# Sums of PV kept feature-major through DRAM for seven of eight branch segments of a gated mix of two infini-attentions

## The chip, the cores and the metric

The kernel runs on one core of a Trainium2 chip. The metric is the device time of one execution in microseconds (us); the median of several executions is compared. TensorE (PE in the profile, PEld for its weight loads) multiplies matrices into eight PSUM banks of 128 partitions by 512 floats. VectorE (DVE), ScalarE (ACT) and GpSimd (POOL) work element by element. SyncE (SP) issues every transfer between DRAM and on-chip memory (SBUF); sixteen DMA engines carry them out. Each engine works through its own queue in the written order and waits on semaphores.

## The reference, cut to what matters

Two branches, A and B, do the same with their own weights on the same x (2048 tokens, 640 features, 32 heads of 20). The tokens are cut into four segments of 512. In a segment every head has causal attention; from the second segment on a memory part is mixed in, built from the keys and values of the segments before.

```python
for s in range(N):                       # N = 4 segments, L = 512
    qs, ks, vs = q[:, :, s], k[:, :, s], v[:, :, s]
    logits = einsum("bhqd,bhkd->bhqk", qs, ks) * scale + mask
    p = softmax(logits)
    a_dot = einsum("bhqk,bhkd->bhqd", p, vs)
    pq = phi(qs)
    num = einsum("bhld,bhde->bhle", pq, M)
    den = einsum("bhld,bhd->bhl", pq, z)[..., None] + 1e-6
    o = g * (num / den) + (1.0 - g) * a_dot          # g = sigmoid(beta), per head
    pk = phi(ks)
    M = M + einsum("bhld,bhle->bhde", pk, vs)
    z = z + einsum("bhld->bhd", pk)
out_branch = concat(o) @ wo
...
g = sigmoid((x * gate_w).sum(-1))        # per token
return g * out_A + (1 - g) * out_B
```

## The kernel before

A **branch segment** t = 0 to 7 is one segment of one branch: t // 2 is the segment s, t % 2 the branch. Its work on TensorE is 10 projections for q and k (one per 128 features, `job_qk`), the projection of v in two halves (`job_v`), the attention of eight units of four heads each (unit i = 8t + u), and five output projections (`job_o`). q, k, v and o weights and their inputs are split in a high and a low part, and three products (high by high, low by high, high by low) stand for one in full precision.

TensorE's array is used as two halves of 64 rows. A planner in the Python code keeps a clock of its own for both halves and for the other engines, and writes the instructions in the order in which it starts them. Projections are the filling (`fill_gen` walks through the list `jobs`); the scores of a unit are strewn in by `RULES`, a table with a row of numbers for each of 66 steps: the order of score pieces (S: queries by keys, for the maxima; T: keys by queries, for the exponentials), how far they spread over the step, how loaded VectorE may be before late work is put off, and waits. The list of late units (`late`) holds turns and the memory's products.

For one unit the chain is: maxima of S in VectorE (line 1109), turned and sent into the query tile; T with the maxima in two more rows; exponential in ScalarE (line 1204); causal cut in GpSimd (1205); then `pv_unit` (line 1232), which multiplies v with the exponentials. Its bank holds, for each of four heads, 20 rows of sums and one row with the denominator, by 512 tokens: features stand in partitions, so it is **feature-major**. The bank is copied to a row tile (line 1259). A row tile is one of 28 places of 128 by 512 floats, shared by all.

Then `fin_unit` turns that tile to tokens: eight transposes on TensorE (line 838, four per half, against an identity), after which tokens stand in partitions. There the denominator of a head is one column, so VectorE multiplies it by the gates (`gq`, 128 by 4 by 32 for a branch segment, line 1298), inverts it (1299) and multiplies the sums (1300). In segment 0 this goes straight into the tile `O` of finished tokens; later the memory part already stands in `O` (`mem_unit`, 800 to 817), and GpSimd adds (1310). When the units that a group of 128 features needs are done, `o_transpose` turns them back to feature-major with eight more transposes (line 838 again, input `O`), and the high and low parts for the output projection are made from the bank (1328). The output of branch A goes to DRAM as `part`, and branch B's is added to it.

The order of jobs in the window of t is: the rest of q, k and v of t, the five output projections of t − 1, then the first five projections of t + 1.

Of the kernel before, what the change touches and what calls it, by code (L numbers as in the profile page):

```python
# [12 lines left out]
F32 = mybir.dt.float32  # L13
# [5 lines left out]
P = 128  # L19
# [23 lines left out]
def tile_gated_mix_infini_attn(  # L43
# [376 lines left out]
    def window_jobs(t):  # L420
        got = [(t, kind, m) for kind, m in (TAIL if t else [("q", 1), ("k", 1), ("v", 0), ("q", 2), ("k", 2)] + TAIL[2:])]
        if t > 0:
            got += [(t - 1, "o", m) for m in range(KT)]
        if t < 7:
            got += [(t + 1, kind, m) for kind, m in HEAD]
# [1185 lines left out]
```

## Time and profile before

| what | us |
|---|---|
| median of three runs | 1027.75 |
| lowest and highest | 1026.51, 1028.1 |
| the profiled execution's own time | 1026.22 |
| span of its profile | 1024.5 |
| TensorE busy | 1015.8 |
| VectorE, ScalarE, GpSimd busy | 760.0, 659.3, 581.5 |

The span is the time from the first to the last instruction of the profiled execution. Busy times of the engines overlap. In a group's row, the number before the bar counts instructions; behind it stand the busy time in us and the mean of one in ns, and then the idle time of that engine just before them with what ended it. In rows of waits stand the waiting engine and line, what it waited for, the total, the times and the longest. In the rows of stretches, the share of the DMA engines and GB/s come last, after the granted clock. In the timeline the start and the length come first; a name such as `bank<-ident,O` is written tile and read tiles.

### The profile page before, as it was taken

What the parts mean: (1) busy time and instruction counts of PE and PEld (TensorE: products, weight loads), DVE (VectorE), ACT (ScalarE), POOL (GpSimd) and SP (SyncE); (2) the same over time, 40 slices, a digit from 0 to 9 for tenths busy, and PEclk for the clock granted to TensorE, in tenths of its full rate; (3) what the DMA queues carried; (4) which work ended last, traced back from release to release, by engine and by line L of the source; (5) the groups of instructions that cost most, each with busy time, mean ns of one, the idle gap of its engine ahead of it and who ended that gap; (6) DMA issues with size and microseconds to landing.
All of it is one profiled execution on the core that took longest, in us unless ns stands there. A gap on an engine that the chain in (4) does not pass through costs nothing.

```text
span 1024.5 us, 31917 instructions
## 1 busy us (share of the span) xinstructions
PE 1015.8 (99%) x11780; PEld 873.7 (85%) x11780; DVE 760.0 (74%) x2725; ACT 659.3 (64%) x1337; POOL 581.5 (57%) x1043
## 2 busy tenths in 40 slices
PE   9999999999999999999999999999999999999998
PEld 7988888988988889889898988989889888888876
DVE  4777787678768788676887668967687867778764
ACT  6375777677655675675756458566675656666672
POOL 4364655665444765566646456565774646645561
PEclk9999999999999999999999999999999999999999
DMA  8996866666675676764766468684775865957431
GB/s 274 305 281 186 280 191 211 194 187 219 181 225 163 196 247 197 232 177 145 264 175 221 132 189 276 196 249 140 205 245 157 263 187 164 286 160 225 134 109 53
DMA packets 110028, 207.97 MB, mean 203 GB/s; under 512 B 12464, under 2 KB 16560, under 8 KB 109872
## 3 DMA queue, kind: packets, MB, share of 16 engines
q1 hardware_dynamic: 109872, 205.93, 66.4%
q8 instruction: 93, 1.52, 0.6%
q14 instruction: 63, 0.52, 0.2%
HBM read 131.43 MB, written 73.40 MB: 200 GB/s over the span
## 4 chain that ended last, share of the span: by engine, by line
PE 95%; DMA 2%; DVE 1%; ACT 1%; POOL 0%; issue 0%; SPq 0%; ACTq 0%; DVEq 0%
PE bank L690 54%; PE bank L1232 13%; PE bank L1122 7%; PE bank L1212 7%; PE bank L838 4%; PE bank L800 3%; PE bank L878 3%; DMA qd<-row 2%; PE bank L1147 1%; PE bank L736 1%; PE bank L328 1%; DMA wst<-in_a_wo_dram 1%; PE bank L1051 0%; DVE bank L1109 0%; DVE row L1036 0%
## 5 line engine op out<-in xcount | busy, mean ns | idle before, releaser
L1109 DVE CUSTOM_DVE_ANT_0 bank<-bank,tri 128x256 f32<-128x256 f32 (+3 forms) x1024 | 475.2, 519 | 135.3 <-PE bank L1122 107.6
L690 PE MATMUL bank<-row,wh 64*128 64x512 f32 x2308 | 528.3, 404 | 0.0
L1204 ACT ACTIVATE p<-bank 128x512 f32<-128x512 f32 x596 | 328.7, 601 | 142.0 <-PE bank L1212 110.1
L1205 POOL TENSOR_SCALAR_AFFINE_SELECT p<-p 128x256 f32<-128x256 f32 (+1 forms) x596 | 215.5, 371 | 228.3 <-ACT p L1204 214.7
L690 PEld LDWEIGHTS bank<-row,wh 64*128 64x128 f32 x2308 | 330.0, 186 | 8.9 <-issue 0.6
L690 PE MATMUL bank<-row,wl 64*128 64x512 f32 x1154 | 308.7, 399 | 0.0
L517 POOL TENSOR_TENSOR wl<-wst,wh 128x640 fp32r<-128x640 f32 x115 | 179.8, 1566 | 81.8 <-ACT wh L515 81.0
L690 PE MATMUL bank<-wvh,row 64*128 64x320 f32 x1280 | 198.4, 316 | 0.1
L690 PEld LDWEIGHTS bank<-row,wl 64*128 64x128 f32 x1154 | 180.3, 186 | 4.4
L1122 PE MATMUL bank<-kst,qst 60*128 60x384 f32 (+3 forms) x1024 | 176.8, 318 | 1.3 <-ACT row L1259 0.6
L1212 PE MATMUL bank<-qst,kst 62*128 62x384 f32 (+3 forms) x1024 | 173.1, 318 | 0.2 <-ACT row L854 0.2
L690 PEld LDWEIGHTS bank<-wvh,row 64*128 64x128 f32 x1280 | 161.3, 185 | 3.1 <-issue 1.0
L1232 PE MATMUL bank<-p,vst 128*32 128x512 f32 (+3 forms) x1952 | 148.3, 429 | 0.0
L1109 DVE DVE_READ_ACCUMULATOR2_ANT mx<- 128x1 f32 x1024 | 144.2, 141 | 0.0
L1122 PEld LDWEIGHTS bank<-kst,qst 60*128 60x128 f32 x1024 | 131.1, 185 | 8.6 <-DVE mx L1109 1.3
L1212 PEld LDWEIGHTS bank<-qst,kst 62*128 62x128 f32 x1024 | 128.9, 186 | 6.8 <-DVE mx L1109 1.0
L1232 PEld LDWEIGHTS bank<-p,vst 128*32 128x32 f32 x1952 | 59.3, 109 | 85.1 <-issue 65.3
L515 ACT CAST wh<-wst 128x640 fp32r<-128x640 f32 x119 | 86.4, 743 | 37.6 <-PE bank L690 26.2
L690 PE MATMUL bank<-wvl,row 64*128 64x320 f32 x640 | 109.9, 311 | 0.0
L690 PEld LDWEIGHTS bank<-wvl,row 64*128 64x128 f32 x640 | 87.7, 185 | 0.3
L492 POOL TENSOR_TENSOR wvl<-wst,wvh 128x640 fp32r<-128x640 f32 (+1 forms) x48 | 64.1, 1341 | 17.1 <-ACT wvh L489 16.5
L838 PE MATMUL bank<-ident,row 64*128 64x64 f32 x752 | 72.7, 225 | 0.8 <-ACT row L1204 0.8
(100 smaller groups left out, 1224.5 us busy)
## 6 DMA issues: line engine op xcount, KB each, us to landing
qd<-row SPq DMA_DIRECT2D x120, 256.0 KB
kd<-row SPq DMA_DIRECT2D x120, 256.0 KB
qst<-qd SPq DMA_DIRECT2D x128, 240.0 KB
kst<-kd SPq DMA_DIRECT2D x128, 240.0 KB
wst<-in_a_wq_dram SPq DMA_DIRECT2D x20, 320.0 KB
wst<-in_a_wk_dram SPq DMA_DIRECT2D x20, 320.0 KB
wst<-in_b_wq_dram SPq DMA_DIRECT2D x20, 320.0 KB
wst<-in_b_wk_dram SPq DMA_DIRECT2D x20, 320.0 KB
```

Of the source, the lines that this page charges most:

```text
L492: put("G", 0.77 * n, lambda: nc.gpsimd.tensor_tensor(out=wl[:, a:b, :], in0=w3, in1=r32(wh[:, a:b, :]), op=ALU.subtract), end, prio=4)
L515: put("A", 0.625, lambda: nc.scalar.copy(wh, w3), lambda: put(lo_eng, lo_cost, lambda: lo.tensor_tensor(out=wl, in0=w3, in1=r32(wh), op=AL ...
L517: lambda: lo.tensor_tensor(out=wl, in0=w3, in1=r32(wh), op=ALU.subtract), end, prio=3), prio=6)
L690: return nc.tensor.matmul(bank_of, lhsT=w[ROWS[half]], rhs=x_[ROWS[half]], start=start, stop=stop)
L800: return nc.tensor.matmul(pm[:, a - h0:c - h0, :].rearrange("p h e -> p (h e)"), lhsT=r32(pqTs[t, m][ROWS[half], P * n:P * (n + 1)]), rhs= ...
L838: return nc.tensor.transpose(px[:, n, r], block(n)[r], ident[r, r])
L1109: put("D", w / 960.0 + 0.105, lambda: nc.vector.tensor_tensor_reduce(out=sc[:, off:off + w], in0=sc[:, off:off + w], in1=tri[:, L - w:], s ...
L1122: lane_ops[half].append((mm(w), lambda pair=pair, qb=qb, off=off, w=w, r=r, sc=sc: nc.tensor.matmul(sc[:, off:off + w], lhsT=q[r, pair, P ...
L1204: put("A", 0.483, lambda: nc.scalar.activation(pt, sc, AF.Exp, scale=SCALE), lambda: (bank.give(sc), put("G", 0.15 + 0.105 * len(todo), la ...
L1205: "G", 0.15 + 0.105 * len(todo), lambda: nc.gpsimd.affine_select(out=blocks, in_=blocks, pattern=[[0, len(todo)], [1, P]], base=0, channel ...
L1212: lane_ops[half].append((mm(w), lambda pair=pair, kb=kb, off=off, w=w, r=r, sc=sc: nc.tensor.matmul(sc[:, off:off + w], lhsT=k[r, pair, P ...
L1232: nc.tensor.matmul(po[32 * j:32 * j + 32, P * kb:], lhsT=vst[t % 2][:, kb, h * E1:h * E1 + 32], rhs=pts[i, n, f][0][:, off:off + w], start ...
```

## The change

For t = 0 to 6 the sums are not turned to tokens. `send_dot` sends the tile of a unit to DRAM while it is feature-major: four transfers of 20 rows to `dots` and one of the four denominator rows to `dens`. When four units (16 heads) are there, `reciprocals` loads their denominators as 128 partitions by 64, multiplies by the head's factor (`gcol`, one number per partition) and the token gate (`row_gate`, laid out in the same way by three small transfers for each branch segment), inverts, and sends them back to `recs`. One transfer from DRAM to DRAM (`wide`) repeats every head's row 20 times, so that it lies as the features do. `mix` loads a tile of 128 features from `dots` and from `wide` and multiplies them, on VectorE or GpSimd. In segment 0 the high and low parts are made of the product at once. In later segments the memory part, which is still made by tokens, is turned by `o_transpose`, and VectorE adds it to the product. The last branch segment (t = 7) works as before.

Beside that, the gates by tokens for the sums (`gqd`) are made for t = 7 only; the first two projections of t + 1 stand ahead of the output projections of t − 1; a second wait (`wait2`) is in the table of rules for the second half of a turn; and the table has new rows.

```diff
@@ RULES (most rows of the table differ; one of them)
-        0: "TSTSTSTSTS 0.969 2.38 0.27 8 0.0 1.6",
+        0: "STTSTSSTST 0.902 2.38 0.24 8 0.0 0.78 1",
...
+    dots = [dram.tile([D, L], F32, name=f"dots{i}") for i in range(7)]
+    dens = [dram.tile([H, L], F32, name=f"dens{i}") for i in range(7)]
+    recs = [dram.tile([H, L], F32, name=f"recs{i}") for i in range(7)]
+    wide = [dram.tile([D, L], F32, name=f"wide{i}") for i in range(7)]
...
     def window_jobs(t):
+        ahead = [(t + 1, kind, m) for kind, m in HEAD] if t < 7 else []
+        got += ahead[:2]
         if t > 0:
             got += [(t - 1, "o", m) for m in range(KT)]
-        if t < 7:
-            got += [(t + 1, kind, m) for kind, m in HEAD]
+        got += ahead[2:]
...
+    def row_gates(s):
+        for b in range(2):
+            t = 2 * s + b
+            if t < 7:
+                row_store.want(1, lambda r, t=t, b=b, s=s: dma(0.3, lambda: nc.sync.dma_start(
+                    out=rowg[t].rearrange("n p -> p n")[:, :, None], in_=gate[b][:, NB * s:NB * (s + 1), None]),
+                    lambda: spread(r, t), prio=8 if s == 0 else marks[16 * s] - 10, some=True), prio=t)
...
             def end():
                 bank.give(po)
+                if t < 7:
+                    send_dot(i, oT)
+                    return
                 oTs[i] = oT
                 later(1, 0.44, lambda: fin_ok(i), lambda: fin_unit(i))
...
+        one = then_all(5, sent)
+        dma(0.1, lambda: nc.sync.dma_start(out=dens[t][4 * u:4 * u + 4, :], in_=oT[DH::32, :]), one, prio=-1)
+        for j in range(4):
+            dma(0.12, lambda j=j: nc.sync.dma_start(
+                out=dots[t][80 * u + DH * j:80 * u + DH * (j + 1), :], in_=oT[32 * j:32 * j + DH, :]), one, prio=-1)
...
+    def reciprocals(t, g, d):
+        rows = slice(16 * g, 16 * g + 16)
...
+        def work():
+            nc.vector.scalar_tensor_tensor(
+                out=d, in0=d, scalar=gcol[t % 2][:, g:g + 1], in1=row_gate[t], op0=ALU.mult, op1=ALU.mult)
+            nc.vector.reciprocal(d, d)
+
+        def written():
+            dma(0.1, lambda: nc.sync.dma_start(
+                out=recs[t][rows, :].rearrange("h (a n) -> (h a) n", n=SPAN), in_=d), widen, prio=-1)
+
+        def widen():
+            dn_store.give(d)
+            dma(1.8, lambda: nc.sync.dma_start(
+                out=wide[t][DH * 16 * g:DH * 16 * (g + 1), :].rearrange("(h e) n -> h e n", e=DH),
+                in_=recs[t][rows, None, :].to_broadcast([16, DH, L])), over, prio=-1)
...
+    def mix(t, k, y, r):
+        def weighed():
+            big.give(r)
+            if t < 2:
+                parts()
+            else:
+                mixed[t, k] = y
+                later(1, 0.44, lambda: all(
+                    (t, n, h) in mem_done for n in range(NB) for h in range(2) if k in mem_tiles(h)), lambda: o_transpose(t, k, parts))
...
+        landed = then_all(2, lambda: anyof(
+            2, weighed,
+            D=(0.605, lambda: nc.vector.tensor_tensor(out=r32(y), in0=r32(y), in1=r32(r), op=ALU.mult)),
+            G=(1.25, lambda: nc.gpsimd.tensor_tensor(out=r32(y), in0=r32(y), in1=r32(r), op=ALU.mult))))
+        dma(0.7, lambda: nc.sync.dma_start(out=r32(y), in_=dots[t][P * k:P * k + P, :]), landed, prio=0)
+        dma(0.7, lambda: nc.sync.dma_start(out=r32(r), in_=wide[t][P * k:P * k + P, :]), landed, prio=0)
```

How it moves instructions is seen best at three places of the built programs. The first is TensorE behind the last PV unit of t = 1. Before, its sums, `row_5270_4569`, are turned into `bank_119` among score pieces (L1122, L1212) and products (L690):

```order
L1122 MATMUL bank_124<-kst_85,qst_81 128x128
L838 MATMUL bank_119<-ident,row_5270_4569 128x64 x2
L690 MATMUL bank_122<-row_3093_2719,wh_132 128x512
L838 MATMUL bank_119<-ident,row_5270_4569 128x64 x2
L690 MATMUL bank_118<-row_3043_2668,wh_128 128x512
L690 MATMUL bank_122<-row_3465_3070,wh_132 128x512
L690 MATMUL bank_118<-row_3093_2719,wh_128 128x512
L1212 MATMUL bank_121<-qst_83,kst_87 128x384
L1212 MATMUL bank_117<-qst_83,kst_87 128x384
L1212 MATMUL bank_121<-qst_83,kst_87 128x128
L838 MATMUL bank_119<-ident,row_5270_4569 128x64 x2
L1212 MATMUL bank_117<-qst_83,kst_87 128x128
```

In the change, the last two rows of that PV unit (now L1261, bank_169) are followed by the memory's update (L907), products (L717) and score pieces (L1241), and no turn reads that unit's sums anywhere:

```order
L1261 MATMUL bank_169<-p_5796_4593,vst_89 32x128
L1261 MATMUL bank_169<-p_5797_4594,vst_89 32x128
L907 MATMUL bank_166<-vst_88,row_5409_4236 128x147
L717 MATMUL bank_168<-row_3412_2767,wh_180 128x512
L907 MATMUL bank_166<-vst_88,row_5409_4236 128x147
L1241 MATMUL bank_163<-qst_80,kst_84 128x512
L1241 MATMUL bank_167<-qst_80,kst_84 128x512
L717 MATMUL bank_168<-row_3444_2785,wh_180 128x512
L907 MATMUL bank_166<-vst_88,row_5409_4236 128x147
```

Eight turns of that unit are gone from the queue, and the bank that they wrote is not taken. The second place is VectorE near the end of t = 1. Before, it weighs a unit's turned sums into the tokens `O_144` between two pairs of maxima (L1109, each with the read of its result):

```order
L1109 ISA bank_122,mx_4888<-bank_122,tri 128x512
L1109 ISA mx_4888 128x1
L901 COPY mt_146<-bank_121 128x147
L1298 TENSOR_TENSOR fw_4937<-bank_124,gqd_141 128x16
L1299 RECIPROCAL fw_4937<-fw_4937 128x16
L1300 TENSOR_TENSOR O_144<-bank_124,fw_4937 128x4x80
L1109 ISA bank_118,mx_4888<-bank_118,tri 128x384
```

In the change, at the end of t = 0, the products of `mix` (L1375) and a low part (L1370) stand there, ahead of the maxima (now L1138):

```order
L1138 ISA mx_3046 128x1
L1375 TENSOR_TENSOR row_3913_3163<-row_3913_3163,row_3914_3164 128x512
L922 COPY mbd_3_78<-bank_164 128x147
L1375 TENSOR_TENSOR row_3918_3165<-row_3918_3165,row_3919_3166 128x512
L1370 TENSOR_TENSOR row_4028_3234<-row_3913_3163,row_4027_3233 128x512
L1138 ISA bank_164,mx_3252<-bank_164,tri 128x512
```

What VectorE waited for there came from TensorE's turn; what it waits for now comes from two transfers. The third place is SP at the same end of t = 0, in the change alone (before, no transfer belongs to this step):

```order
L1306 DMA dens_125<-row_3710_3017 4x512
L1308 DMA dots_118<-row_3710_3017 20x512 x4
L1341 DMA wide_138<-recs_131 320x1x512
L532 DMA wst_173<-in_a_wo_dram 128x640
L554 DMA row_3845_3124<-in_xT_dram 128x512
L554 DMA row_3876_3142<-in_xT_dram 128x512
L611 DMA rowg_148<-gate_91 128x4x1
L1377 DMA row_3913_3163<-dots_117 128x512
L1378 DMA row_3914_3164<-wide_138 128x512
L1377 DMA row_3918_3165<-dots_117 128x512
L1378 DMA row_3919_3166<-wide_138 128x512
```

The loads of sums and widened factors stand behind the widening, and weights, inputs of the next segment and the first sums of t = 1 share the queue with them.

More of the change, by code (lines that the diff above doesn't have):

```diff
@@ L824, in end @@
             mem_done.add((t, n, h))
+            if t < 7 and all((t, nn, hh) in mem_done for nn in range(NB) for hh in range(2)):
+                gq_store.give(gq.pop(t))
         def read():
@@ new lines, in reciprocals, with landed, over @@
+    def reciprocals(t, g, d):
+        rows = slice(16 * g, 16 * g + 16)
+        def landed():
+            put("D", 0.75, work, written, prio=2)
+        def work():
[10 more added lines that the diff above has]
+                in_=recs[t][rows, None, :].to_broadcast([16, DH, L])), over, prio=-1)
+        def over():
+            rec_there.add((t, g))
+            if (t, 1 - g) in rec_there:
+                row_store.give(row_gate.pop(t))
+            dots_ready(t)
+        dma(0.1, lambda: nc.sync.dma_start(
+            out=d, in_=dens[t][rows, :].rearrange("h (a n) -> (h a) n", n=SPAN)), landed, prio=-1)
@@ L1287, in end @@
             fin_done.add(i)
-            if all(8 * t + j in fin_done for j in range(8)):
-                gq_store.give(gq.pop(t))
             for k in range(KT):
@@ L1317, in tile_gated_mix_infini_attn, with o_transpose, add @@
     ot_count = {}
-    def o_transpose(t, k):
+    def o_transpose(t, k, parts=None):
         b = bank.free.pop(0)
         px = b.rearrange("p (n c) -> p n c", c=P)
+        def add():
+            y = mixed.pop((t, k))
+            put("D", 0.605, lambda: nc.vector.tensor_tensor(
+                out=r32(y), in0=b, in1=r32(y), op=ALU.add), lambda: (bank.give(b), parts()), prio=2)
         def got(hi, lo):
@@ L1444, in lane_step @@
         u = seconds[half][0] if seconds[half] else None
[L1445 removed]
+        if u and next_start(half, u["ops"][half][0][0][1])[1] >= u["at"] + (rule["wait2"] if u["turn"] else 0.0):
             return run_second(half, u)
@@ L1512, in rules @@
         if i in RULES:
-            order, rule["span"], rule["calm"], rule["lag"], rule["room"], rule["hold"], rule["wait"] = RULES[i].split()
+            order, rule["span"], rule["calm"], rule["lag"], rule["room"], rule["hold"], rule["wait"], rule["wait2"] = RULES[i].split()
             rule.update({x: float(rule[x]) for x in rule if x != "order"}, order=order)
```

76 lines of the change are left out of this document (59 added, 17 removed), and 111 rows, old and new, of the table RULES.

## The prediction

> **What bounds the kernel now.** I read the page's first part, then the chain that ended last, then the stretches, then who waited for whom.
>
> ```profile
> PE 1015.8 (99%) x11780; PEld 873.7 (85%) x11780; DVE 760.0 (74%) x2725; ACT 659.3 (64%) x1337; POOL 581.5 (57%) x1043
> PE 95%; DMA 2%; DVE 1%; ACT 1%; POOL 0%; issue 0%; SPq 0%; ACTq 0%; DVEq 0%
> by line: PE bank L690 54.1%; PE bank L1232 13.5%; PE bank L1122 7.1%; PE bank L1212 6.9%; PE bank L838 4.4%; PE bank L800 3.1%; PE bank L878 3.0%; DMA qd<-row 1.6%; PE bank L1147 0.8%; PE bank L736 0.7%; PE bank L328 0.6%; DMA wst<-in_a_wo_
> ```
>
> TensorE is busy 99% of the span and its own work makes 95% of the chain. A matmul's record overlaps its neighbours', so 99% alone proves little; the list of TensorE's waits says more.
>
> ```profile
> PE bank L328 <- DVE qst L332: 1.5, 1, 1.5
> PE bank L838 <- ACT row L1204: 0.8, 1, 0.8
> PE bank L1122 <- ACT row L1259: 0.6, 1, 0.6
> PE bank L1122 <- DVE row L854: 0.5, 1, 0.5
> PE bank L1212 <- ACT row L854: 0.2, 1, 0.2
> PE bank L1122 <- ACT p L1204: 0.2, 1, 0.2
> ```
>
> That is the whole list: under 4 us in six waits, and no transfer is in it. The stretches show the same from beginning to end, at full clock.
>
> ```profile
> 0.00:100.00 100.00, 97.67 (x1002) 84.56 (x1004) 67.97 (x233) 57.37 (x116) 50.08 (x84) 1.00 0.86 265
> 100.00:200.00 100.00, 100.00 (x1222) 87.10 (x1222) 74.42 (x273) 71.67 (x148) 60.58 (x116) 1.00 0.73 222
> 200.00:1024.50 824.50, 818.11 (x9563) 702.05 (x9559) 617.58 (x2224) 530.22 (x1074) 470.88 (x845) 1.00 0.64 193
> ```
>
> So the number and price of TensorE's instructions set the time. What leaves its queue shortens the span, as long as what replaces it doesn't make it wait.
>
> **What is removed from TensorE.** A unit of turns is eight transposes, four per row half. Gone are the 56 units that turned PV's sums to tokens (seven of eight branch segments, eight groups of heads each) and ten that turned the finished tokens back in branch segments 0 and 1. Branch segments 2 to 6 still turn their memory part. That is 66 × 8 = 528 of these 1072 rows:
>
> ```profile
> L838 PE MATMUL bank<-ident,row 64*128 64x64 f32 x752 | 72.7, 225 | 0.8 <-ACT row L1204 0.8
> L838 PEld LDWEIGHTS bank<-ident,row 64*128 64x128 f32 x752 | 60.7, 138 | 3.7 <-ACT row L1204 1.1 <-issue 0.8 <-PE bank L838 0.3
> L838 PE MATMUL bank<-ident,O 64*128 64x64 f32 x320 | 34.4, 226 | 0.1
> L838 PEld LDWEIGHTS bank<-ident,O 64*128 64x128 f32 x320 | 27.9, 139 | 3.8 <-issue 2.3 <-PE bank L838 0.5 <-DVE row L657 0.2
> L690 PEld LDWEIGHTS bank<-row,wh 64*128 64x128 f32 x2308 | 330.0, 186 | 8.9 <-issue 0.6 <-ACT row L674 0.4 <-PE bank L690 0.3
> 170.19 0.41 PE L838 MATMUL bank<-ident,O 64*128 64x64 f32 x4
> 170.41 0.39 PE L690 MATMUL bank<-wvh,row 64*128 64x320 f32 x1
> 170.43 0.39 PE L690 MATMUL bank<-row,wh 64*128 64x512 f32 x1
> ```
>
> Three prices. The lowest is the bare slot: in the timeline four turns of one half start at 170.19 and the next products at 170.41 and 170.43, so four take 0.24 us of their half at most, and both halves lose that once: 66 × 0.24 = 15.8 us. The middle is what the chain charges: 4.4% of 1024.5 us is 45.1 us for 1072 turns, 0.042 us each, and 528 × 0.042 = 22.2 us. It holds the time that a turn costs its neighbours as well. The highest counts weight loads: (60.7 + 27.9) × 528 / 1072 = 43.6 us of PEld's 873.7. I take the chain's 22.2, because it alone is measured along what sets the end, and keep 15.8 and 43.6 for the range.
>
> **What the other engines gain and lose.**
>
> ```profile
> L1298 DVE TENSOR_TENSOR fw<-bank,gqd 128x16 f32<-128x16 f32 x64 | 10.9, 171 | 19.7 <-PE bank L838 12.5 <-ACT row L1204 2.9 <-PE bank L1122 1.4
> L1299 DVE RECIPROCAL fw<-fw 128x16 f32<-128x16 f32 x64 | 16.2, 253 | 2.5 <-DVE fw L1298 0.4
> L1300 DVE TENSOR_TENSOR ft<-bank,fw 128x320 f32<-128x320 f32 x48 | 23.6, 492 | 4.8 <-DVE fw L1299 0.5
> L1328 DVE TENSOR_TENSOR row<-bank,row 128x512 fp32r<-128x512 f32 x40 | 27.5, 688 | 15.1 <-ACT row L1328 12.4 <-POOL mt L1134 2.6
> L539 DVE TENSOR_TENSOR row<-row,row 128x512 fp32r<-128x512 f32 x5 | 3.4, 692 | 0.9 <-ACT row L535 0.9
> L539 POOL TENSOR_TENSOR row<-row,row 128x512 fp32r<-128x512 f32 x15 | 19.3, 1298 | 2.3 <-ACT row L535 2.1
> L1310 POOL TENSOR_TENSOR O<-O,ft 128x320 f32<-128x320 f32 x46 | 40.9, 890 | 30.9 <-DVE ft L1300 26.7 <-DVE mw L814 4.1
> ```
>
> VectorE loses 56 × (171 + 253 + 492) ns = 51.3 us of weighing and 35 × 0.688 = 24.1 us of low parts read from a bank. It gets 54 of the 70 new whole-row operations (35 products, 35 low parts) at 0.692 us, 37.4 us; 25 additions of the memory part, 17.2 us; and 14 inversions of 128x64, about 0.17 us for the product and some 0.54 us for the reciprocal (an estimate: 253 ns for 16 columns against 241 for 13 in the same view gives near 5 ns a column), 10 us. The net is some 10 us less. GpSimd loses 40 additions, 35.6 us, and gets 16 whole-row operations at 1.298 us, 20.8 us. ScalarE casts the same 35 tiles from another place. None of them is near TensorE's share, so I cost this at nothing; if it were all on the path it would be a gain, not a loss.
>
> **What is added in transfers.** 417 more (893 become 1310), all issued by SP. In bytes, from the shapes: 9.2 MB of sums written, 9.2 read back, 9.2 of widened factors written and 9.2 read, 1.6 of small ones: 38.4 MB.
>
> ```profile
> q1 hardware_dynamic: 109872, 205.93, 66.4%
> L1038 SPq DMA_DIRECT2D out_dram<-row x5: 332/333/338, 1018.0 to 1020.7; - x5
> L979 SPq DMA_DIRECT2D out_dram<-row x15: 337/349/413, 324.2 to 854.5; - x15
> 281.84 2.29 PE bank L1232 x32
> 14.73 3.66 PE bank L690 x30
> ```
>
> At the same price per byte the queue's share goes from 66.4% to 66.4 × 244.3 / 205.9 = 79%; in the stretch 100 to 200, some 5 MB more takes 0.73 to near 0.88, close to the 0.86 that the first stretch bore. Issuing adds 417 × 0.35 = 146 us to SP, which waits for much of the span. So bandwidth should hold; the length of the path is the question. After a segment's last PV come five transfers in a row: sums and denominators out, denominators in as 128x64, the inverse out, widened in memory, both back in. One transfer of 256 KB takes at most 3.8 us to land (the last is issued at 1020.7, the span ends at 1024.5). Five make 19 us; four more issues, the wider third and the six tiles that hang on the second group of heads add some 8, VectorE's and ScalarE's steps 3: about 30 us. The room for it: branch segment 1's last PV ends at 284.1 (281.84 + 2.29) and its first finished output leaves at 324.2, 40 us later; of that the job's own 30 products take at least 3.7 us. The change puts two jobs of 30 products ahead, 7.3 us more at the price of 3.66 us for 30; their two weight tiles go ahead of the output weights on SP too, in the order in which TensorE needs them. So some 43 us of room at most against 30.
>
> The Trainium skill's page "DMA: Bandwidth & Descriptors", section "Anatomy of one DMA — SWDGE (gpsimd) path", puts a transfer's fixed cost at about 2.0 us, most of it the receipt of the write, plus bytes over 436 GB/s. By it (an estimate) 256 KB take 2.6 us and the five steps 13 us instead of 19, and the chance that the path is late would be smaller than I put it; the section fits another issuing path, and no row of before shows one small transfer alone.
>
> Waiting is what can go wrong. The inversion and the product sit in in-order queues ahead of the maxima (L1109) that free the score banks. Before, these groups waited for transfers:
>
> ```profile
> L515 ACT CAST wh<-wst 128x640 fp32r<-128x640 f32 x119 | 86.4, 743 | 37.6 <-PE bank L690 26.2 <-DMA wst<-in_b_wo_dram 3.0 <-DMA wst<-in_a_wq_dram 2.3
> L489 ACT CAST wvh<-wst 128x640 fp32r<-128x640 f32 (+1 forms) x48 | 31.0, 651 | 5.3 <-DMA wst<-in_b_wv_dram 3.7 <-DMA wst<-in_a_wv_dram 1.5
> L1259 ACT COPY row<-bank 128x512 f32<-128x512 f32 x59 | 34.8, 590 | 55.9 <-PE bank L1232 47.6 <-PE bank L878 3.2 <-DMA qd<-row 2.5
> L854 DVE COPY row<-bank 128x512 f32<-128x512 f32 x8 | 5.5, 691 | 10.0 <-DMA qd<-row 4.4 <-PE bank L1147 2.2 <-PE bank L838 1.6
> ```
>
> They add up to 17.4 us, or 0.0195 us for each of 893 transfers; 417 more make 8 us of engine time, of which VectorE's idle quarter and the banks in reserve hide most. I take 3 us on the path. The bounds are 0 and, at 28 places (14 inversions, 14 groups of products) with 1 us each uncovered, 28 us.
>
> **The table of rules** is new in most rows and moves the order of everything; no row of before prices that. I give it nothing and 5 us either way.
>
> **The sum.** The profiled execution took 1026.22 us (span 1024.5). 1026.22 − 22.2 + 3 = 1007.0. The median of the three runs is 1.5 us above the profiled one, so 1008.5.
>
> **The rivals.**
> - *A larger gain.* Turns cost the products around them more than the chain shows, by holding up their weight loads. For it: the 43.6 us of loads that go. Against it: a product's load is 186 ns beside a slot of 0.122 us, a turn's 138 ns beside 0.06 us in its half, so loads overlap. Between 22.2 and 43.6 I put this case at 33 us saved: 1026.2 − 33 + 3 + 1.5 = 998.
> - *Weight loads are the bound.* Then all 43.6 us come off: 1026.2 − 43.6 + 1.5 = 984. PEld's 85% beside a TensorE that waits for nobody speaks against it. The Trainium skill's page "Trainium Kernel Development and Optimization", section "Best Practices", says that distance to the limit is judged by the busy share of LDWEIGHTS and not by that of matmuls; by that rule this would be the case.
> - *Part is given back.* The path of five transfers is later than its room in each of seven branch segments, by 1.5 us: 10.5 us, about 1019. For it: nothing before is that long. Against it: 43 us against 30; it begins to cost at 1.4 times my path.
> - *Slower.* VectorE stands at the inversion or the product until a transfer lands, the maxima queue behind it, score banks stay taken, TensorE stops. At 28 places it breaks even from 22.2 / 28 = 0.8 us each; at 1.1 us uncovered it costs 31 us: 1026.2 − 22.2 + 31 + 1.5 = 1036. For it: the queue's share near 0.88 early, SP in order with 417 more entries, each able to hold those behind. Against it: 17.4 us of such waits before, none that reached TensorE.
> - *It changes nothing*: the turns' slots were filled anyway by waiting. Against it: six waits on TensorE in all. 1027.
>
> **Chances.** Forecast 0.60 (1000 to 1015), larger gain 0.09, weight loads 0.02, part given back 0.13, no change 0.03, slower 0.13. A measurement of this kernel tells 0.2%, some 2 us, from no change. Faster 0.84, same 0.03, slower 0.13. The range of eight in ten goes from 997 (just under the larger gain) to 1022 (past the partial one): about 0.06 is left out below and 0.14 above.
>
> **What would show it.** Right: TensorE's list still names no transfer, L838's successor has 544 rows and about 23 us of chain, the share of PE in the chain stays above 93%, the queue's share is near 79%. Wrong: TensorE waiting for L1138 (the maxima's new line) or for rows that come from transfers, VectorE's idle time ahead of the inversions and products in tens of us, or stretches in which TensorE's count of instructions falls just where the output projections begin.

## The result, and the profile after

The changed kernel takes 1106.09 us (median of four, 1103.16 to 1109.64) where the kernel before took 1027.92 beside it (1026.51 to 1028.59). The ratio is 1.0764, 95% interval 1.073 to 1.0798: slower, by 78 us, and 98 us above the forecast.

First the page of the changed kernel: span, busy times, packets, the transfer queue (packets, MB, share) and the chain that ended last.

```profile
span 1104.7 us, 31255 instructions
PE 1035.1 (94%) x11252; PEld 877.9 (79%) x11252; DVE 770.5 (70%) x2636; ACT 657.6 (60%) x1334; POOL 574.0 (52%) x1010
DMA packets 142027, 246.50 MB, mean 223 GB/s; under 512 B 26208, under 2 KB 30304, under 8 KB 141872
q1 hardware_dynamic: 141872, 244.50, 75.3%
PE 30%; DMA 6%; DVE 2%; ACT 1%; POOL 1%; issue 1%; SPq 0%; DVEq 0%; ACTq 0%; POOLq 0%
```

TensorE has the 528 instructions fewer that were promised (11,252 for 11,780), but it made 95% of the chain and now makes 30%. Its list of waits, six entries and 3.8 us before, has 28 entries and 64.4 us; its first rows (what waited, for what, total us, times, longest):

```profile
PE bank L1241 <- ACT p L1233: 9.3, 2, 6.3
PE bank L867 <- DVE row L668: 8.3, 1, 8.3
PE bank L1151 <- DVE mx L1138: 5.4, 4, 3.3
PE bank L827 <- ACT vst L957: 4.6, 1, 4.6
```

These are few and long, and entries further down name GpSimd and a transfer too: no one engine is late, several are, for some us at a time. The stretches show when. Two us each: length, TensorE's busy time with its instructions, its granted clock, the DMA engines' share and their GB/s.

```profile
480.00:482.00 2.00, 2.00 (x29) 1.00 1.06 402
482.00:484.00 2.00, 2.00 (x29) 1.00 0.40 148
484.00:486.00 2.00, 2.00 (x36) 1.00 0.31 47
486.00:488.00 2.00, 2.00 (x32) 1.00 0.37 39
488.00:490.00 2.00, 1.48 (x24) 1.00 0.46 8
490.00:492.00 2.00, 0.00 (x0) 0.98 0.47 32
492.00:494.00 2.00, 0.00 (x0) 0.50 0.58 38
494.00:496.00 2.00, 1.89 (x16) 0.50 0.80 235
...
502.00:504.00 2.00, 2.00 (x18) 0.50 1.05 288
```

For ten us the DMA engines move 8 to 47 GB/s in the place of 400, while 31 to 58% of their time is still taken; then TensorE runs dry, and its granted clock is 0.50 until behind 504. Such a stop costs more than its own length. The mean granted clock over the execution is 0.964 (0.999 before), and by the trace TensorE worked some 60 us at 0.50, which is 30 us lost at full clock. Its busy time shows it: 1035.1 us for 11,252 instructions, where the run E5 below, at full clock, needs 996.3 for as many. So of the 96 us by which the changed kernel's span is longer than that run's (1104.7 for 1009.2), some 39 are slower work and the rest is idle time.

SyncE's timeline (start, length) says what was issued at that moment:

```profile
483.17 0.39 SPq L611 DMA_DIRECT2D rowg<-gate  x1
483.78 0.56 SPq L1306 DMA_DIRECT2D dens<-row  x1
484.38 1.58 SPq L1308 DMA_DIRECT2D dots<-row  x4
486.00 0.34 SPq L1377 DMA_DIRECT2D row<-dots  x1
486.39 0.44 SPq L1378 DMA_DIRECT2D row<-wide  x1
494.16 0.32 SPq L1377 DMA_DIRECT2D row<-dots  x1
```

`rowg<-gate` is the first of the three small gate transfers: 128 partitions with four numbers each, written to memory as 512 pieces of four bytes, 2 KB in all. Behind it SyncE stands for 7.3 us. But a want of issued work does not explain the hole: two loads of 256 KB were issued at 486.00 and 486.39, and from 486.8 to 494 all sixteen engines moved 0.16 MB. In the trace's records of single pieces none begins between 487 and 489, and pieces of 2 KB, which took 84 ns at 480 to 482 (the median), take up to 4.1 us around that gap. SyncE's list of waits has this kind of transfer at three lines:

```profile
SPq L1308 <- DMA rowg<-gate: 7.5, 2, 3.9
SPq L1377 <- DMA rowg<-gate: 7.3, 1, 7.3
SPq L616 <- DMA rowg<-gate: 6.4, 3, 3.6
```

L1308 and L1377 have nothing to do with gates. They wait because of how the program numbers its transfers: each takes one of eight semaphores in turn and waits until the transfer before it on the same semaphore has landed. The written order of SyncE shows it at the fifth `rowg` (the suffix on the semaphores is the same on all):

```
554 L611 DMA rowg_149<-gate_90 128x4x1 [waits DMAHW2_49,DVE_49]
...
561 L1188 DMA qst_81<-mr_196 2x8x128 [waits DMAHW1_49]
562 L1308 DMA dots_119<-row_8711_6838 20x512 [waits DMAHW2_49]
```

So at most eight transfers of SyncE are under way, and one that lands late holds all behind it.

### The profile page after: what moved, and what is told of

Its sections match the earlier page's. It is cut to its first block, busy times and chain, and to the rows that moved or that the text cites. A ratio compares the mean times of both kernels' runs of the same rounds, so it can differ in the third digit from the quotient of the medians.

```text
span 1104.7 us, 31255 instructions
## 1 busy us (share of the span) xinstructions
PE 1035.1 (94%) x11252; PEld 877.9 (79%) x11252; DVE 770.5 (70%) x2636; ACT 657.6 (60%) x1334; POOL 574.0 (52%) x1010
## 3 DMA queue, kind: packets, MB, share of 16 engines
q1 hardware_dynamic: 141872, 244.50, 75.3%
## 5 line engine op out<-in xcount | busy, mean ns | idle before, releaser
L1138 DVE CUSTOM_DVE_ANT_0 bank<-bank,tri 128x256 f32<-128x256 f32 (+3 forms) x1024 | 474.4, 520 | 168.7 <-PE bank L1151 119.7
L717 PE MATMUL bank<-row,wh 64*128 64x512 f32 x2308 | 504.6, 408 | 2.4 <-ACT mr L1193 1.7
L1233 ACT ACTIVATE p<-bank 128x512 f32<-128x512 f32 x580 | 319.3, 599 | 140.0 <-PE bank L1241 110.9
L717 PEld LDWEIGHTS bank<-row,wh 64*128 64x128 f32 x2308 | 325.6, 189 | 14.8 <-ACT mr L1193 2.6
L717 PE MATMUL bank<-row,wl 64*128 64x512 f32 x1154 | 295.0, 403 | 0.0
L1241 PE MATMUL bank<-qst,kst 62*128 62x384 f32 (+3 forms) x1024 | 185.8, 324 | 18.7 <-ACT p L1233 9.3
L717 PE MATMUL bank<-wvh,row 64*128 64x320 f32 x1280 | 184.9, 320 | 0.3 <-DVE row L1291 0.3
L717 PEld LDWEIGHTS bank<-row,wl 64*128 64x128 f32 x1154 | 176.1, 188 | 4.8
L1241 PEld LDWEIGHTS bank<-qst,kst 62*128 62x128 f32 x1024 | 138.2, 190 | 25.8 <-ACT p L1233 11.0
L717 PEld LDWEIGHTS bank<-wvh,row 64*128 64x128 f32 x1280 | 151.5, 190 | 2.6 <-issue 1.0
L1261 PE MATMUL bank<-p,vst 128*32 128x256 f32 (+3 forms) x1912 | 151.0, 434 | 1.6 <-DVE mx L1138 0.9
L1138 DVE DVE_READ_ACCUMULATOR2_ANT mx<- 128x1 f32 x1024 | 144.5, 141 | 0.0
L1261 PEld LDWEIGHTS bank<-p,vst 128*32 128x32 f32 x1912 | 60.3, 111 | 87.8 <-issue 60.9
L717 PE MATMUL bank<-wvl,row 64*128 64x320 f32 x640 | 98.4, 313 | 0.0
L717 PEld LDWEIGHTS bank<-wvl,row 64*128 64x128 f32 x640 | 79.7, 188 | 0.1
L684 DVE TENSOR_TENSOR row<-bank,row 128x512 fp32r<-128x512 f32 x80 | 54.1, 685 | 24.5 <-ACT row L701 15.2
```

The costliest lines, as they stand in the source:

```text
L684: put("D", 0.605, lambda: nc.vector.tensor_tensor(out=lo, in0=src, in1=r32(hi), op=ALU.subtract), out, prio=1)
L717: return nc.tensor.matmul(bank_of, lhsT=w[ROWS[half]], rhs=x_[ROWS[half]], start=start, stop=stop)
L1138: put("D", w / 960.0 + 0.105, lambda: nc.vector.tensor_tensor_reduce(out=sc[:, off:off + w], in0=sc[:, off:off + w], in1=tri[:, L - w:], s ...
L1233: put("A", 0.483, lambda: nc.scalar.activation(pt, sc, AF.Exp, scale=SCALE), lambda: (bank.give(sc), put("G", 0.15 + 0.105 * len(todo), la ...
L1241: lane_ops[half].append((mm(w), lambda pair=pair, kb=kb, off=off, w=w, r=r, sc=sc: nc.tensor.matmul(sc[:, off:off + w], lhsT=k[r, pair, P ...
L1261: nc.tensor.matmul(po[32 * j:32 * j + 32, P * kb:], lhsT=vst[t % 2][:, kb, h * E1:h * E1 + 32], rhs=pts[i, n, f][0][:, off:off + w], start ...
```

## The experiments

Two theories at first. **Theory 1:** the small scatters land some 10 us late and stop the other transfers; by way of the queue of eight (form a) or by clogging the DMA engines (form b). **Theory 2:** the path of five transfers, by its length or load. Times are medians, ratios are to the kernel before in the same session, with the 95% interval.

**E1, larger pieces.**

```diff
- out=rowg[t].rearrange("n p -> p n")[:, :, None], in_=gate[b][:, NB * s:NB * (s + 1), None]
+ out=rowg[t].rearrange("n p -> (n p)").rearrange("(p n) -> p n", n=NB), in_=gate[b][:, NB * s:NB * (s + 1)]
```

> The changed kernel, but the gate columns go to the memory buffer as 128 pieces of 16 bytes instead of 512 pieces of 4 bytes (the token order of the row gates is then permuted, so the output is not the reference's); the small beta scatter at the start stays as it is. Theory 1 (each four-byte scatter lands some 10 us after its issue and stops everything that SyncE issues behind it): the scatters then land in some 3 to 4 us, the steps of 8 to 12 us behind seven of them go, and the time falls from 1106 to some 1045 us, the step at the start remaining. Theory 2 (the path of five transfers and their number make the loss, as VectorE and GpSimd wait for the wide and row tiles): nothing changes there, some 1100 us.

1072.51 us, 1.0439 [1.0405, 1.0473]: 34 us come back. In its stretches around the same scatter (issued at 456.34) the hole is 4 us, not 10, and TensorE does not stop in them:

```profile
456.00:458.00 2.00, 2.00 (x29) 1.00 0.64 219
458.00:460.00 2.00, 2.00 (x35) 1.00 0.38 89
460.00:462.00 2.00, 2.00 (x33) 1.00 0.85 276
```

The gain is theory 1's, but the time lies between the two forecasts.

**E2, the scatter alone in the kernel before.**

```diff
+ nc.sync.dma_start(out=rowg[t].rearrange("n p -> p n")[:, :, None], in_=gate[b][:, NB * s:NB * (s + 1), None])   # t = 0..6, behind segment_gate
```

> The kernel before, with seven scatters of 512 four-byte pieces added behind the gates of the segments, issued by SyncE into buffers that nothing reads; nothing else is changed. Theory 1: each stops SyncE's later transfers for some 8 to 10 us, and with less slack around them than the changed kernel has lost here or there, the time rises from 1027 to some 1085 us (7 times some 8). Theory 2: 3,584 small pieces that nobody waits for cost nothing, 1027 to 1030 us.

1046.02 us, 1.0181 [1.0147, 1.0215]. Seven scatters that nobody reads cost 19 us, 2.7 each: theory 2 is refuted for them, and my 8 us each was too much where there is slack.

**E3, no small gate transfers.**

```diff
- dma(0.3, lambda: nc.sync.dma_start(out=rowg[t]..., in_=gate[b]...
+ dma(0.3, lambda: None,                     # rows_g, rg, cols_g and gcol alike; gate tiles set to 1.0
```

> The changed kernel without the small gate transfers: the scatters of token gates and betas and the readings behind them are left out, and the tiles that they fill are set to one at the start, so that the token gates and head factors of the seven segments' sums are missing from the output. The five transfers of denominators and recips, and the order that the planner writes, stay. Theory 1: the 75 us that were lost in steps behind the scatters go, 1010 to 1030 us. Theory 2: 1095 to 1100 us.

1053.10 us, 1.0250 [1.0184, 1.0316]. All small gate transfers together cost 53 of the 98 us, and neither theory alone holds: 45 us above 1008.5 remain.

**E4, the scatters on another queue.**

```diff
- nc.sync.dma_start(out=rowg[t]... ; nc.sync.dma_start(out=cols_g[b]...
+ nc.gpsimd.dma_start(out=rowg[t]... ; nc.gpsimd.dma_start(out=cols_g[b]...
```

> The changed kernel with the scatters of token gates and betas issued by GpSimd in the place of SyncE; the readings behind them stay with SyncE. If the loss comes from SyncE's queue, in which the transfers behind a slowly landing scatter must wait for it (theory 1, form a), the steps go but for what the readings themselves wait: some 1030 to 1045 us. If the scatter clogs the DMA engines themselves for some 10 us (theory 1, form b), the time stays near 1100 us. Theory 2: also near 1100 us.

1098.89 us, 1.0696 [1.0658, 1.0734]: only 7 us come back. SyncE's waits for a `rowg` to land fell from 21.2 us to 8.5, all of them now at the reading behind the scatter, so form a is small and form b makes most of the loss. The view of the tile `rowg` has GpSimd's issuing (ns) and the landing:

```profile
L611 POOL DMA_DIRECT2D rowg<-gate x7: 762/767/808, 92.9 to 724.9; - x7
DMA to landing us min/median/max: 11.6/11.9/12.2
```

The stretches behind its fifth scatter, with the columns as before:

```profile
446.00:448.00 2.00, 2.00 (x31) 1.00 0.94 242
448.00:450.00 2.00, 2.00 (x29) 1.00 1.44 108
450.00:452.00 2.00, 2.00 (x22) 1.00 0.71 81
452.00:454.00 2.00, 0.71 (x8) 1.00 0.91 123
454.00:456.00 2.00, 0.34 (x6) 1.00 0.31 90
```

2 KB take 11.9 us to land, and for ten us from 448 on the engines move 81 to 123 GB/s for everybody, where they moved 242 just before; TensorE stops here too. The Trainium skill's page "DMA: Bandwidth & Descriptors", section "Issuing engines are not separate DMA queues", says that transfers run on the same sixteen engines whoever starts them; this run agrees. Its "Specifications" put the least piece for full rate at 512 bytes and name a read-modify-write below it; E1's pieces of 16 bytes lie below that too, so no run here tests that limit or the read-modify-write, and no figure of that section comes near 11.9 us.

**E5, no transfers of the path either.** From here on the base is E3.

```diff
- nc.sync.dma_start(out=dens[t]...), dots, dn, recs, wide, row<-dots, row<-wide
+ None
- nc.vector.tensor_tensor(out=r32(y), in0=r32(y), in1=r32(r), op=ALU.mult)
+ nc.vector.tensor_tensor(out=r32(y), in0=gw[:, :L], in1=gw[:, :L], op=ALU.mult)
```

> The kernel without small gate transfers (1053 us), and now also without the path's own transfers: denominators, sums, recips and widened tiles are not moved, the inversion reads a tile of ones, and the product multiplies two constant tiles into the row tile, so the seven segments' sums are missing from the output. Every computation's count and the written order stay. If the 417 transfers and their 38 MB make the rest of the loss: 1005 to 1012 us, which is the prediction without its added waits. If the written order of the rest (the changed table of rules, stalls at the maxima) makes it: still 1040 to 1055 us.

1010.78 us, 0.9843 [0.9814, 0.9871]. TensorE is the bound again; the page's busy times:

```profile
PE 996.3 (99%) x11252; PEld 851.7 (84%) x11252; DVE 769.5 (76%) x2636; ACT 656.3 (65%) x1334; POOL 577.4 (57%) x1017
```

Its longest wait in sum is 1.9 us:

```profile
PE bank L1151 <- DVE mx L1138: 1.9, 3, 1.4
```

So 16.2 us of the forecast's 19.2 us of gain are there, and transfers take all of it and more.

**E6, fewer bytes, E7, more transfers.**

```diff
E6:
- in_=recs[t][rows, None, :].to_broadcast([16, DH, L])
+ in_=recs[t][rows, None, :P].to_broadcast([16, DH, P])          # dots, row<-dots, row<-wide alike
E7:
- nc.sync.dma_start(out=dots[t][80 * u + DH * j:80 * u + DH * (j + 1), :], ...
+ [nc.sync.dma_start(out=dots[t][80 * u + DH * j + c:80 * u + DH * j + c + DH // 2, :], ... for c in (0, DH // 2)]
```

> The kernel without small gate transfers (1053 us), with as many transfers of the path but only the first 128 of 512 columns in the sums', the widened and the two row transfers (rows of 512 bytes in the place of 2,048; denominators and recips stay whole; the product reads constants and the quarter's recips, so the sums are missing from the output). Some 28 MB are moved less. If bytes (the share of the transfer queue) make the rest of the loss: some 1015 us. If the number of transfers, each taking a place among those that SyncE may have under way, makes it: 1045 to 1053 us.

> The kernel without small gate transfers (1053 us), with each of the 224 transfers of sums to memory issued as two of ten rows: the same bytes and the same pieces, 224 transfers more. If the number of transfers makes the rest of the loss, 417 having cost some 45 us over the predicted 1008, then 224 more cost some 20 us or more: 1073 to 1085 us. If bytes make it: within 5 us of 1053.

E6: 1030.49 us (eight executions, 1026.43 to 1037.09), 1.0045 [1.0014, 1.0076], between its two forecasts. The queue's rows of E3 and of E6 have the same pieces and 28 MB less:

```profile
q1 hardware_dynamic: 135856, 244.02, 75.2%
q1 hardware_dynamic: 135856, 216.50, 70.4%
```

That gives 23 of the 42 us between E3 and E5. E7: 1128.80 us, 1.0992 [1.0883, 1.1101]: 224 transfers more with the same bytes cost 76 us, far beyond the forecast of 1073 to 1085. Both cost, and the number costs more than I thought. In E7 SyncE waits at a sum's store for landings that it has nothing to do with, by the rotation of eight; its list of waits:

```profile
SPq L1308 <- DMA kst<-kd: 14.9, 28, 1.3
SPq L1308 <- DMA qst<-qd: 8.8, 13, 1.5
```

Each issue takes it 0.33 us (the view of the tile `dots`: least, median and largest ns):

```profile
L1308 SPq DMA_DIRECT2D dots<-row x448: 272/328/2019, 68.9 to 1012.8; - x150
```

The 224 more take 73 us of SyncE's time by that, so its issuing is a rival to the rotation of eight; E7 does not divide the two.

**E9, E10 and E13, another issuer for the 280 stores of sums and denominators.**

```diff
- nc.sync.dma_start(out=dens[t]... ; nc.sync.dma_start(out=dots[t]...
+ nc.scalar.dma_start(...                                    # E9
+ nc.gpsimd.dma_start(...                                    # E10; E13: dots in halves of ten rows too
```

> The kernel without small gate transfers (1053 us), with the 280 transfers of sums and denominators to memory issued by ScalarE in the place of SyncE; same transfers, same bytes, same places among those under way at once (token gates and head factors are missing from the output as there). If SyncE's own queue makes the number's part of the loss (0.36 us of issuing each, 594 us in all, and the transfers behind one that waits for its tile), it falls to some 1025 to 1035 us. If the limit is the number of transfers under way at once, or bytes: 1050 to 1065 us, ScalarE waiting in SyncE's place.

> The same with these 280 transfers issued by GpSimd, whose transfers have places of their own (the scatter's issue took it 0.77 us, so some 215 us of its time, 577 to 790 us). If the limit is the number of SyncE's transfers under way, this falls to some 1030 us and the kernel with ScalarE's queue does not. If SyncE's own queue is the limit, both fall, this one less, by GpSimd's 215 us (1030 to 1050 us). If bytes alone: 1050 us or more.

> The kernel without small gate transfers, with 448 half transfers of sums and 56 of denominators to memory issued by GpSimd (token gates and head factors are missing from the output). On SyncE's queue the halving cost 75 us (1053 to 1129). If the limit is the number of SyncE's transfers under way, the halving costs here only GpSimd's own time, 224 times 0.51 us = 115 us of which its idle time hides the most (716 of 1036 us are busy): 1041 to 1060 us. If a transfer more costs the same on any queue (the engines that carry it out): some 1110 us.

E9: 1087.18 us, 1.0584 [1.0554, 1.0615], beyond both forecasts. ScalarE's transfers take the same eight semaphores in the same rotation, so the two queues share the eight places. SyncE waits longer at L1188 (for `kst<-kd` 28.0 us, in E3 5.7), and ScalarE's exponentials (L1233) stand behind its own stores; two rows of SyncE's list and one of ScalarE's:

```profile
SPq L1188 <- DMA kst<-kd: 28.0, 11, 5.4
SPq L1188 <- DMA qst<-qd: 27.2, 11, 5.9
ACT p L1233 <- DMA dots<-row: 20.6, 10, 3.3
```

E10: 1041.30 us, 1.0138 [1.0059, 1.0216]. GpSimd's have eight semaphores of their own: 12 us gained (two executions each: 1037.9 and 1044.7, in E3 1050.6 and 1055.6), although GpSimd is busy 716 us for 577. E13: 1086.61 us, 1.0586 [1.0504, 1.0667]. Halving costs 45 us here against 76 on SyncE's queue, neither forecast. GpSimd is 76% busy and its own work is late:

```profile
PE bank L1176 <- POOL mt L1163: 7.4, 7, 1.6
PE bank L1261 <- POOL p L1234: 3.1, 6, 0.7
```

E9 relieves SyncE of the same issuing as E10 but adds no places, and loses; so the places under way are likely part of the number's price. The issuer's own time is likely part of it too. Neither was changed alone, and how the two divide stays open.

**E15 and E17, who waits for the path.** In E3, VectorE waits 31.2 us in 21 waits for the path's loads and TensorE 16.4 us for VectorE's maxima, which is the prediction's slower rival at work. VectorE's two rows:

```profile
DVE row L1375 <- DMA row<-wide: 16.9, 13, 3.5
DVE dn L1331 <- DMA dn<-dens: 14.3, 8, 3.8
```

E15 puts inversions and products later; E17 keeps order, number and bytes of the transfers and lets nobody wait for the loads (those of sums and denominators now end in DRAM, not in SBUF).

```diff
E15:
- dma(0.7, lambda: nc.sync.dma_start(out=r32(r), in_=wide[t]...), landed, prio=0)
+ dma(0.7, lambda: nc.sync.dma_start(out=r32(r), in_=wide[t]...), landed, prio=0, lat=4.0)   # dots and dens alike
E17:
- nc.sync.dma_start(out=r32(y), in_=dots[t][P * k:P * k + P, :])
+ nc.sync.dma_start(out=away0[t][P * k:P * k + P, :], in_=dots[t][P * k:P * k + P, :])       # dens alike; product of constants as in E5
```

> The kernel without small gate transfers (1053 us), with the planner told that the path's three loads land 2.9 us later, so that inversions and products stand later in the queues of VectorE and GpSimd (what depends on them moves too; token gates and head factors are missing from the output as there). If VectorE's standing at them makes the rest of the loss: its waits on the path's loads fall from 31.2 us to under 10, and the time to some 1025 to 1040 us. If the other transfers' lateness makes it: the waits fall, the time stays at 1045 to 1060 us.

> The kernel without small gate transfers (1053 us), same order, same number and bytes of transfers, but no engine waits for the path's loads: the sums and denominators are loaded into memory that nothing reads, the inversion reads a tile of ones, the product two constant tiles (so the sums are missing from the output). If VectorE's and GpSimd's standing at inversions and products (31 and 14 us of waits) makes the rest of the loss: some 1015 to 1025 us. If the crowding of the transfers themselves makes it (weights, query and key tiles and maxima late behind them): 1043 to 1053 us.

E15: 1071.78 us, 1.0435 [1.0405, 1.0465]. VectorE's waits for the loads fell to 8.2 us and TensorE's for the maxima to 3.9, yet the time rose by 19, beyond both forecasts: the written order changed too, so this run decides nothing. E17: 1046.97 us, 1.0197 [1.012, 1.0275], 6 us below E3 and hardly outside the spread of both (1043.7 to 1050.2, 1050.6 to 1055.6). So the standing of VectorE and GpSimd at the path's loads makes some 6 of the 42 us, by the ends of both spreads 0 to 12; what is left must be what the transfers do to other work. One engine that waits then is seen in ScalarE's list of waits in E3, where it casts weights and inputs:

```profile
ACT wvh L500 <- DMA wst<-in_b_wv_dram: 15.3, 12, 3.2
ACT row L546 <- DMA row<-in_xT_dram: 15.2, 13, 3.7
ACT wvh L500 <- DMA wst<-in_a_wv_dram: 8.9, 8, 3.0
```

Summed over its rows for weights and inputs this is 20.4 us in the kernel before, 21.7 in E5, 40.2 in E6, 43.9 in E10, 60.8 in E3 and 91.6 in E7, which is nearly the order of these times. But others stand out of it: E17 has 72.3 at 1047 us, E9 only 27.5 at 1087 and E16 41.3 at 1081. No run took this wait away by itself, and it is not shown to be the cause.

**E8, E11 and E14, gates without transfers, all outputs computed.** E8 makes the gate rows with planned TensorE units. E11 keeps the order and puts the products where the scatters stood. E14 is E11 with E10's stores.

```diff
E11:
- nc.sync.dma_start(out=rowg[t]..., then rows_g, then rg
+ for n in range(NB):
+     nc.tensor.matmul(px[:, P * n:P * (n + 1)], lhsT=gate[b][:, NB * s + n:NB * s + n + 1].to_broadcast([P, P]), rhs=ident, start=True, stop=True)
+ nc.vector.tensor_tensor(out=pa, in0=pa, in1=own8[:, :, None].to_broadcast([P, 8, SPAN]), op=ALU.mult)
+ nc.vector.tensor_reduce(out=r, in_=px.rearrange("p (a n) -> p n a", n=SPAN), axis=mybir.AxisListType.X, op=ALU.add)
E8:
+ later(1, 0.2, lambda: True, lambda: row_unit(t, r, w))      # one product of a spread gate tile with the identity
```

> The changed kernel computing all that it should, without any small gate transfer: the token gates of a segment are spread to head-and-token rows by one small TensorE product (a gate tile spread by GpSimd against the identity) and a VectorE copy, seven times, and the head factors by a masked sum on VectorE at the start. Theory 1 at the size that the two kernels without gate transfers gave: 1045 to 1060 us, 46 to 60 less than the changed kernel. If those kernels were faster only because something depended on the left-out values' arrival: near 1090 us.

> The changed kernel computing all that it should, its order kept, with each scatter and the two readings behind it replaced at the scatter's place by four TensorE products of a gate column with the identity and two VectorE instructions, and the head factors by a masked sum at the start. If the 1079 us of the kernel with planned gate units came from its other order: 1053 to 1062 us (the kernel without gate transfers, and seven times some 1 us). If making the gates on the chip costs that much by itself: some 1075 us.

> The changed kernel computing all that it should, with the gates made in place and the 280 transfers of sums and denominators issued by GpSimd. If the parts add: 1065 - 12 = 1053 us, still slower than before by the path's bytes and reads. If gates in place and the busier GpSimd stand in each other's way: 1060 us or more.

E8: 1078.98 us, 1.0507 [1.0476, 1.0537]. E11: 1065.30, 1.0371 [1.0312, 1.043], 3 us above its forecast and 12 above E3. E8, 14 us slower, is beyond its forecast of 1045 to 1060; its other order is the likely reason, but it also makes the gates in another way. E14: 1045.73, 1.0187 [1.01, 1.0274]: 60 us better than the change and the best of the changed kernels that compute everything, but still slower than before.

**E12 and E16** are E11 with E9's stores and E14 with E15's delay.

> The kernel with gates made in place, and the 280 transfers of sums and denominators issued by ScalarE, computing all that it should. With the first theory of SyncE's queue: 1025 to 1040 us, near the kernel before (1027). With the limit on transfers under way or bytes: 1055 to 1070 us.

> The same in the kernel that computes all that it should, with gates made in place and sums and denominators sent by GpSimd (1045.7 us; VectorE waits 11.4 us there for the path's loads). If VectorE's standing makes its loss: some 1036 us. If not: 1040 to 1050 us.

1102.22 us, 1.0731 [1.0646, 1.0815], and 1081.20 us, 1.0527 [1.0496, 1.0557], both beyond their forecasts: what lost time alone loses it here too. In E16 VectorE's waits for the path's loads fell from 11.4 us to 0.7 and the time still rose by 35.

## Why the prediction was wrong

**The step that failed** is the one on added transfers. It counted 417 in bytes, share of the queue and SyncE's issuing, concluded "So bandwidth should hold; the length of the path is the question", and priced the rest at 17.4 us of waits over 893 transfers: 3 us on the path. Measured, against E5 where they are absent, they cost 1106 − 1011 = 95 us: 53 the small gate transfers (34 of them by the size of the `rowg` pieces alone), 42 the path, of which some 23 are bytes by E6. The other 19 are what is left with a quarter of the long rows' bytes: the number of transfers, and some us of standing at the loads (E17). Part of all this is TensorE's clock, which the prediction took as full: 30 of the 95 us.

- *The small gate transfers* stood in the sum only inside "1.6 of small ones" megabytes. Their pieces, four bytes each, stood in the diff and were never priced. On the transfer queue they are 0.5 of 38.6 MB (244.50 less 244.02 in E3, and 244.50 less 205.93), and made over half of the loss. Before had no row of such a scatter, and it was given no bound. The bytes themselves came out as forecast (38.4 by shapes), and the queue's share is 75.3%, not 79.
- *The price per transfer* was an average of waits in a kernel whose transfers came in time. The 17.4 us were too few even so: the rows shown name only the three largest releasers of a group, and the lists of waits before give 30.9 us for the three engines (25.1 on ScalarE, 4.4 on VectorE, 1.4 on GpSimd). At that price 417 more make 14 us and not 8, still far from 42. Issuing time was 146 us for 417 by the prediction; that SyncE's transfers are under way eight at a time, so that a new one can hold up weights and query tiles, was not looked for, though the written order shows it.
- *Removed from TensorE* held: 544 turns are left as said, and E5 is 16.2 us faster than before. That fits the bare slot's 15.8 better than the chain's 22.2. But E5 also carries the new table of rules, so 22.2 with a table that costs 6 would give the same, and no run divides them.
- *The weight-load rival* (984), drawn from the Trainium skill's page "Trainium Kernel Development and Optimization", section "Best Practices", is refuted by E5: 528 loads fewer gave 16 us, not 43.6. TensorE is 99% busy there, its loads 84%: read as a sign of what bounds the kernel, that section's rule does not hold here.
- *Other engines cost nothing*: right in effect, though VectorE's busy time went from 760.0 to 769.5 in E5, not down by 10. A whole-row product of two row tiles took 0.85 us in the changed kernel, not 0.69.
- *The table of rules*, 0 ± 5: no run changed it alone. E5, which carries the new table and order, leaves it some 6 us at most beside the chain's price and nothing beside the bare slot's. An order changed in other ways, with that table left as it is, may cost more: E8 is 14 us slower than E11, and E15 19 slower than E3.
- *The slower rival* (1036) got the side right but for the most part not the mechanism. VectorE does stand at the inversions and products (37.2 us in the changed kernel, 25.1 of them for `row<-wide`), and E17 puts such standing at some 6 us of the path's 42. Its remark that SyncE's entries hold those behind them was nearer.
- *What would show it*: TensorE's chain was to stay above 93%; it is 30%. Of the wrong signs named, two came: TensorE waits for the maxima of L1138 (13.1 us in all) and VectorE idles some 37 us ahead of inversions and products. TensorE's long stops came too, but for the most part behind scatters: of its twelve stops over 1.5 us ten begin within 23 us of the issue of a `rowg`.

## What to carry to other kernels

Price a transfer by its pieces and by what it keeps from the others, not by its bytes: seven scatters of 2 KB in four-byte pieces cost more here (34 us by E1, against pieces of 16 bytes) than 28 MB in long rows (23 us by E6). Count a stop of TensorE at more than its length, for its clock fell behind it. Where one queue issues everything and a fixed number may be under way, look in the written order at which transfer waits for which, and count new ones against it. And an operation that the old profile never shows needs a bound of its own, even when it looks like nothing.

## What was not expected of the hardware

- A scatter of 512 four-byte pieces to DRAM, issued by GpSimd (E4), took 11.9 us to land and left 81 to 123 GB/s for everybody for ten us; issued by SyncE, in the changed kernel, it left 8 to 47 GB/s for ten us. 128 pieces of 16 bytes left a hole of 4 us (E1).
- After a stop of TensorE of some 4 us the granted clock was 0.50 for some 13 us (492 to 505 in the changed kernel). With its other stops this cost some 30 us of that kernel's work.
- A store of 20 rows cost its issuer 0.33 us on SyncE (E3, and as much with ten rows in E7) and 0.51 on GpSimd (E10), and from GpSimd it landed in 1.8 to 6.4 us.
